# ScalarE's order of copies, exponentials and outputs in a decode attention kernel

## The chip, the cores and the metric

The kernel runs on one core of a Trainium2 chip. The metric is the time on the device in microseconds (us), the median of several runs. A core has engines that run side by side, each working through its own instructions in order: TensorE (PE in the profile), VectorE (DVE), ScalarE (ACT), GpSimd (POOL) and SyncE (SP), which here only issues transfers. They wait for each other through semaphores. Transfers between the chip's main memory and the core's own memory are made by 16 DMA engines.

## What is computed

One query for each of 16 heads attends to 8192 keys of width 256, all in bfloat16:

```python
B, H, Sq, Sk, D = 1, 16, 1, 8192, 256
scale = q.shape[-1] ** -0.5
scores = jnp.einsum("bhqd,bhkd->bhqk", q, k) * scale
p = _softmax(scores, axis=-1)
return jnp.einsum("bhqk,bhkd->bhqd", p, v)
```

K and V are 4 MiB a head each, 128 MiB (134.2 MB) together, and each is read once.

## The kernel before

A head's 8192 keys lie on 128 partitions, 64 keys to a partition, so K and V of a head are a tile of 128 x 64 columns of 256 numbers. There are two buffers for K and two for V, one for even and one for odd heads. SP issues the transfers in a fixed list (line 57): after the first heads always K of head h+2 and then V of head h. K of head h+2 waits until DVE and PE are through with K of head h (lines 132, 133); V of head h waits until the sum over V of head h-2 is done (line 135). V of heads 13 to 15 comes in pieces.

The scores of a head are split. DVE does 48 of the 64 columns, each a multiplication with q and a sum (line 189). PE and ACT do the other 16 in four groups of four columns: PE transposes a group (line 278), ACT copies it out of PE's memory (`evac`, line 367), PE multiplies it with q (line 292). `tp` and `KT` have two buffers each, so a group's transposes follow the scores of two groups before. ACT then copies the 16 columns of scores to the rest (`scopy`, line 371).

Around this stand, for each head: DVE's maximum over its columns (line 206), PE's transposition of it (226), DVE's maximum over the partitions (`xmax`, 173), PE's spreading of that over the partitions (`bcast`, 232), ACT's negation and exponential (`expo`, 375 and 379), which also makes the sum of each partition, PE's sum of these over the partitions (`total`, 242), DVE's reciprocal of it (`recips`, 178), PE's 64 multiplications of the weights with V (`pv`, 257), ACT's scaling of the result and the DMA issue of the output (`final`, 392 and 399). `q_copy` (362) lays the next head's q ready for DVE and PE; it waits until DVE is through with the head before, since there are two buffers.

All of it is written out by hand as loops over eight pairs of heads, one loop for each engine, and the order on an engine is the order of the text. PE's turn for the pair (even, odd) is: scores of the even head; pv of the previous even head, with the maximum, spreading and sum of the previous odd head at its columns 32, 48 and 64; scores of the odd head, with the maximum and spreading of the even head in between and its sum at the end; pv of the previous odd head. PE has a ninth turn for the last two pv. ACT's turn is, for the even and then the odd head: first copy, q copy, second copy, (odd head only: exponential of the even head), third and fourth copy, copy of the scores, (even head only: exponential of the previous odd head), and the output of the head two before. DVE's turn is the 48 columns of the even head, with `xmax` of the previous odd head at column 40, and the 48 of the odd head, with the reciprocal of the previous odd head at column 2, `xmax` of the even head at column 3, and the reciprocal of the even head at its end.

Semaphore values are counted from `AHEAD` (line 17), the number of steps that each is set to at the start; `of(1, 2)` is the head's number plus two. Both sums go to the same place (`qps`), and DVE reads it from there.

Of the kernel before, what the change touches and what calls it, by code (L numbers as in the profile page):

```python
# [13 lines left out]
K_FIRST = 16  # L14
V_HALVED = 13
V_LATE = {14: (0, 16, 32, 48), 15: (0, 16, 32, 44, 52, 58, 62)}
AHEAD = {"kd": 1, "sc": 1, "sp": 2, "ex": 2, "m": 1, "g": 1, "mT": 1, "l": 1, "bc": 1, "nb": 1, "rc": 2, "pv": 2, "fin": 4}
V_SEMS = (("va0", "v0b", "v0c", "v0d"), ("va1", "v1b", "v1c", "v1d", "v1e", "v1f", "v1g"))


# [20 lines left out]
def bass_standalone__mha_softmax__decode_kernel(nc: bass.Bass, q: bass.AP, k: bass.AP, v: bass.AP, out: bass.AP):  # L41
# [7 lines left out]
    NG = NPE // GRP  # L49
# [21 lines left out]
    with contextlib.ExitStack() as ctx:  # L71
# [9 lines left out]
        def sem(name):  # L81
            if name not in sems:
                sems[name] = ctx.enter_context(nc.semaphore(name))
            return sems[name]
# [39 lines left out]
        if True:  # L124
# [44 lines left out]
            @(lambda f: f(nc.vector))  # L169
            def _(dve):  # L170
                def xmax(h):
                    dve.wait_ge(sem("mT"), h.of(1, 2))
                    dve.tensor_reduce(g[0:1, h.par : h.par + 1], mx[0:1, 0:P], AX.X, ALU.max).then_inc(sem("g"), 1)  # L173

                def recips(h):
                    dve.wait_ge(sem("l"), h.of(1, 2))
                    dve.wait_ge(sem("fin"), h.of(1, 3))
                    dve.reciprocal(recip[0:1, h.par : h.par + 1], qps[0:1, 0:1]).then_inc(sem("rc"), 1)  # L178

                def head(h, at):  # L180
                    dve.wait_ge(sem("qb"), h.of(1, 1))
                    dve.wait_ge(sem("ex"), h.of(1, 1))
                    dve.wait_ge(sem(f"k{h.par}"), h.of(8, 16 - 8 * h.par))
                    buf = kbuf[h.par]
                    for j in range(JD):
                        if j == K_FIRST and h.par == 0:

                            dve.wait_ge(sem("k0b"), 16)
                        ins = dve.tensor_tensor_reduce(  # L189
                            out=buf[:, j * D : (j + 1) * D],  # L190
                            in0=buf[:, j * D : (j + 1) * D],
                            in1=q_now[h.par][:, 0:D],
                            scale=SCALE,
                            scalar=0.0,
                            op0=ALU.mult,
                            op1=ALU.add,
                            accum_out=S[h.par][:, j : j + 1],
                        )
                        if j in at:
                            at[j]()  # L200
                    ins.then_inc(sem("kd"), 1)
                    if JD in at:
                        at[JD]()
                    dve.wait_ge(sem("kd"), h.of(1, 2))
                    dve.wait_ge(sem("sc"), h.of(1, 2))
                    dve.tensor_reduce(m[:, h.par : h.par + 1], S[h.par][:, :], AX.X, ALU.max).then_inc(sem("m"), 1)  # L206

                with dve.Fori(0, H // 2) as i:
                    ev, od = _Step(0, i), _Step(1, i)
                    prev = od.back(2)  # L210

                    def later(f):
                        with dve.If(i > 0):
                            f(prev)

                    head(ev, {40: lambda: later(xmax)})
                    head(od, {2: lambda: later(recips), 3: lambda: xmax(ev), JD: lambda: recips(ev)})
                last = _Step(H - 1)
                xmax(last)
                recips(last)  # L220

            @(lambda f: f(nc.tensor))
            def _(pe):
# [16 lines left out]
                def total(h):  # L240
                    pe.wait_ge(sem("ex"), h.of(1, 3))
                    pe.matmul(  # L242
                        qps[0:1, 0:1],
                        lhsT=lsum[:, h.par : h.par + 1],
                        rhs=ones_col[:, 0:1],
                        start=True,
                        stop=True,
                    ).then_inc(sem("l"), 1)

                def pv(h, waits, at):  # L250

                    pe.wait_ge(sem("fin"), h.of(1, 3))
                    pe.wait_ge(sem(f"va{h.par}"), h.of(8, 32 - 8 * h.par))
                    for j in range(J):
                        for name, value in waits.get(j, ()):
                            pe.wait_ge(sem(name), value)
                        ins = pe.matmul(  # L257
                            acc[h.par][0:1, 0:D],
                            lhsT=E[h.par][:, j : j + 1],
                            rhs=vbuf[h.par][:, j * D : (j + 1) * D],  # L260
                            start=(j == 0),
                            stop=(j == J - 1),
                        )
                        if j == J - 1:
                            ins.then_inc(sem("pv"), 1)
                        if j + 1 in at:
                            at[j + 1]()
# [33 lines left out]
                def scores(t, before=None):  # L301
                    if before:
                        transpose_m(before)
                    for gi in range(NG):
                        ktrans(t, gi)
                        if gi >= 1:
                            kscore(t, gi - 1)
                        if gi == 1 and before:
                            bcast(before)
                    kscore(t, NG - 1)  # L310
                    if before:
                        total(before)

                pe.wait_ge(sem("ldq"), 16)
                pe.wait_ge(sem("cb"), 1)
# [23 lines left out]
                with pe.Fori(0, H // 2 + 1) as i:  # L339
                    ev, od = _Step(0, i), _Step(1, i)  # L340
                    fin_turn = pe.snap((i // 8) * 16 + 16)
                    half_turn = pe.snap(((i + 1) // 8) * 16 + 16)
                    old = od.back(2)
                    with pe.If(i < H // 2):
                        scores(ev)
                    with pe.If(i > 0):
                        pv(
                            ev.back(2),
                            {V_LATE[14][n]: [(V_SEMS[0][n], fin_turn)] for n in range(1, len(V_SEMS[0]))},
                            {32: lambda: transpose_m(old), 48: lambda: bcast(old), 64: lambda: total(old)},  # L350
                        )
                    with pe.If(i < H // 2):
                        scores(od, before=ev)
                    with pe.If(i > 0):
                        waits = {V_LATE[15][n]: [(V_SEMS[1][n], fin_turn)] for n in range(1, len(V_SEMS[1]))}
                        waits[HALF].append(("v1h", half_turn))
                        pv(old, waits, {})

            @(lambda f: f(nc.scalar))
            def _(act):  # L360
# [3 lines left out]
                def evac(h, gi):  # L364
                    act.wait_ge(sem("tp"), h.of(NG, gi + 1))
                    act.wait_ge(sem("sp"), h.of(NG, gi + 1))
                    act.activation(out=KT[gi % 2][:, :], in_=tp[gi % 2][:, :], func=ACT.Copy).then_inc(sem("kt"), 1)  # L367
# [54 lines left out]
                with act.Fori(0, H // 2) as i:  # L422
                    for c in (0, 1):
                        t = _Step(c, i)
                        evac(t, 0)
                        act.wait_ge(sem("kd"), t.of(1, 1))
                        act.wait_ge(sem("sp"), t.of(NG, 2))
                        q_copy(_Step(c + 1, i), q_all[:, bass.ds(i * (2 * QW) + (c + 1) * QW, QW)])
                        evac(t, 1)
                        if c:  # L430
                            expo(t.back(1))
                        evac(t, 2)
                        evac(t, 3)
                        scopy(t)
                        with act.If(i > 0):
                            if c == 0:
                                expo(t.back(1))
                            done = t.back(2)
                            at = nc.s_assert_within(
                                (i - 1) * (2 * D) + c * D,  # L440
                                0,
                                (H - 1) * D,
                                skip_runtime_bounds_check_because="the branch is taken from turn 1 on",
                            )
                            final(done, flat[:, bass.ds(at, D)])
                expo(_Step(H - 1))
                for h in (H - 2, H - 1):
                    final(_Step(h), out[0, h, 0:1, :])
# [31 lines left out]
```

## Time and profile before

| | |
|---|---|
| time, median of 3 runs | 321.04 us (320.5 to 322.54) |
| time of the profiled execution | 321.04 us |
| its span | 319.6 us |
| PE, DVE, ACT busy | 220.9, 274.9, 92.0 us (69%, 86%, 29%) |
| read from main memory | 134.23 MB, 420 GB/s over the span |
| granted TensorE clock, mean | 0.84 |

The profile is one execution. "Span" is the time from its first to its last instruction; the difference to the time lies around it. Busy time of an engine is an average over stages and does not say what sets the end; for that there are the chain of waits, which goes back from the last instruction to whatever released it each time, and the timeline, with the start and length of each instruction and the idle time before it. The granted clock is the share of TensorE's full clock that it was given. In rows of instructions, "L257" is line 257 of the kernel, "x64" the number of instructions merged into the row, and a pair of brackets the idle time before it and what ended it. SPq and ACTq are the queues that issue.

### The profile page before, as it was taken

Reading aid. Unit: us, or ns where it says so; the run is one execution under the profiler, and the core shown is the slowest. Engines: PE = TensorE matmul, PEld = TensorE weight load, DVE = VectorE, ACT = ScalarE, POOL = GpSimd, SP = SyncE. Lnnn points to the kernel's source line nnn. Section 1 sums busy time; section 2 is a strip of 40 time slices with the busy share of each in tenths; the row PEclk is TensorE's granted clock in tenths of the full one; section 3 lists DMA queues with packets and bytes.
Section 4 is the critical chain, followed back from the end, with each engine's and each line's share of the span. In section 5 each row is a group of like instructions: output and inputs, shape, how many; then the busy total and the mean of one; then the engine's idle time right before and its main releaser. Section 6 shows DMA issues by size and latency. Waiting matters only on the chain.

```text
span 319.6 us, 6845 instructions
## 1 busy us (share of the span) xinstructions
PE 220.9 (69%) x2162; PEld 156.3 (49%) x2162; DVE 274.9 (86%) x1584; ACT 92.0 (29%) x171; POOL 1.6 (0%) x11
## 2 busy tenths in 40 slices
PE   4427186797875947849297573966749477397997
PEld 1326154565554635626256352653626355265675
DVE  2799999999999998897979979889797997979910
ACT  5436050433224060510506123060231605116010
POOL 1000000000000000000000000000000000000000
PEclk9999999769598786969769598785969969587799
DMA  8999999999999999999999999999999999999994
GB/s 329 451 397 455 392 453 416 416 427 435 439 418 443 431 435 439 418 439 427 439 435 423 439 418 443 431 431 435 427 439 414 447 435 427 439 406 423 422 399 179
DMA packets 6549, 134.29 MB, mean 420 GB/s; under 512 B 752, under 2 KB 912, under 8 KB 1424
## 3 DMA queue, kind: packets, MB, share of 16 engines
q1 hardware_dynamic: 6480, 134.22, 98.3%
q8 instruction: 2, 0.03, 0.0%
q10 hardware_dynamic: 64, 0.02, 0.0%
q14 instruction: 3, 0.02, 0.0%
HBM read 134.23 MB, written 0.01 MB: 420 GB/s over the span
## 4 chain that ended last, share of the span: by engine, by line
DMA 49%; PE 24%; DVE 23%; issue 2%; ACT 1%; ACTq 0%; SPq 0%; DVEq 0%
DMA vbuf<-in_v_dram 45%; PE acc L257 23%; DVE kbuf L189 22%; DMA kbuf<-in_k_dram 4%; DVE S L189 1%; PE sm L232 1%; ACT KT L367 1%; PE mx L226 0%; ACT o_sb L392 0%; ACT q_now L362 0%; DVE g L173 0%; SPq L136 0%; PE spe L292 0%; ACTq L399 0%; DVE recip L178 0%
## 5 line engine op out<-in xcount | busy, mean ns | idle before, releaser
L189 DVE CUSTOM_DVE_ANT_0 kbuf<-kbuf,q_now 128x256 bf16<-128x256 bf16 x768 | 268.1, 413 | 22.2 <-DMA kbuf<-in_k_dram 21.2
L257 PE MATMUL acc<-vbuf,E 128*1 128x256 bf16 x1024 | 147.6, 315 | 36.3 <-DMA vbuf<-in_v_dram 36.3
L257 PEld LDWEIGHTS acc<-vbuf,E 128*1 128x1 bf16 x1024 | 96.7, 96 | 80.4 <-DMA vbuf<-in_v_dram 37.3
L367 ACT ACTIVATE KT<-tp 128x1024 bf16<-128x1024 bf16 x64 | 63.8, 1018 | 30.3 <-PE tp L278 30.1
L189 DVE DVE_READ_ACCUMULATOR2_ANT S<- 128x1 f32 x768 | 58.4, 76 | 0.0
L278 PE MATMUL tp<-identb,kbuf 128*128 128x128 bf16 x512 | 42.3, 239 | 13.9 <-DMA kbuf<-in_k_dram 13.8
L292 PE MATMUL spe<-q_now,KT 128*128 128x1 bf16 x512 | 23.1, 166 | 32.3 <-ACT KT L367 31.6
L278 PEld LDWEIGHTS tp<-identb,kbuf 128*128 128x128 bf16 x512 | 33.5, 107 | 18.3 <-DMA kbuf<-in_k_dram 12.4
L292 PEld LDWEIGHTS spe<-q_now,KT 128*128 128x128 bf16 x512 | 18.0, 100 | 42.0 <-ACT KT L367 32.0
L392 ACT ACTIVATE o_sb<-acc,recip 1x256 bf16<-1x256 f32 x16 | 7.4, 464 | 99.9 <-PE acc L257 98.6
L375 ACT ACTIVATE negb<-sm 128x1 f32<-128x1 f32 x16 | 2.8, 172 | 84.5 <-PE sm L232 84.5
L173 DVE TENSOR_REDUCE g<-mx 1x1 f32<-1x128 f32 x16 | 4.4, 276 | 9.8 <-PE mx L226 9.8
L226 PE MATMUL mx<-ident,m 128*1 128x128 f32 x32 | 6.3, 279 | 5.7 <-DVE m L206 5.7
L232 PE MATMUL sm<-g,ones_row 1*128 1x1 f32 x32 | 6.2, 262 | 4.1 <-DVE g L173 4.1
L232 PEld LDWEIGHTS sm<-g,ones_row 1*128 1x128 f32 x32 | 4.9, 190 | 6.2 <-DVE g L173 4.7
L362 ACT ACTIVATE q_now<-q_all 128x258 bf16 (+1 forms) x17 | 7.0, 412 | 0.3 <-DVE S L189 0.3
L178 DVE RECIPROCAL recip<-qps 1x1 f32<-1x1 f32 x16 | 2.4, 151 | 3.9 <-PE qps L242 3.9
L379 ACT ACTIVATE E<-S,negb 128x64 bf16<-128x64 f32 x16 | 5.6, 348 | 0.5
L226 PEld LDWEIGHTS mx<-ident,m 128*1 128x1 f32 x32 | 2.2, 83 | 6.3 <-DVE m L206 5.9
L329 PE MATMUL acc<-q_sb,identb 16*128 16x256 bf16 x16 | 4.4, 403 | 1.0 <-ACT q_all L412 1.0
L371 ACT ACTIVATE S<-spe 128x16 f32<-128x16 f32 x16 | 2.9, 183 | 7.3 <-PE spe L292 7.3
L412 ACT ACTIVATE q_all<-acc 128x512 bf16<-128x512 f32 x8 | 4.4, 593 | 0.9 <-PE acc L329 0.9
(20 smaller groups left out, 16.6 us busy)
## 6 DMA issues: line engine op xcount, KB each, us to landing
kbuf<-in_k_dram SPq DMA_DIRECT2D x15, 4096.0 KB, 20.5
vbuf<-in_v_dram SPq DMA_DIRECT2D x11, 4096.0 KB, 29.0
vbuf<-in_v_dram SPq DMA_DIRECT2D x6, 2048.0 KB, 24.4
vbuf<-in_v_dram SPq DMA_DIRECT2D x6, 1024.0 KB, 12.8
kbuf<-in_k_dram SPq DMA_DIRECT2D x1, 3072.0 KB, 11.7
kbuf<-in_k_dram SPq DMA_DIRECT2D x1, 1024.0 KB, 4.8
vbuf<-in_v_dram SPq DMA_DIRECT2D x1, 768.0 KB, 9.1
vbuf<-in_v_dram SPq DMA_DIRECT2D x1, 512.0 KB, 9.9
```

What stands on the lines that cost most here:

```text
L173: dve.tensor_reduce(g[0:1, h.par : h.par + 1], mx[0:1, 0:P], AX.X, ALU.max).then_inc(sem("g"), 1)
L189: ins = dve.tensor_tensor_reduce(out=buf[:, j * D : (j + 1) * D], in0=buf[:, j * D : (j + 1) * D], in1=q_now[h.par][:, 0:D], scale=SCALE, ...
L226: pe.matmul(mx[0:1, 0:P], lhsT=m[:, h.par : h.par + 1], rhs=ident[:, :], start=True, stop=True).then_inc(sem("mT"), 1)
L232: pe.matmul(sm[:, 0:1], lhsT=ones_row[0:1, 0:P], rhs=g[0:1, h.par : h.par + 1], start=True, stop=True,).then_inc(sem("bc"), 1)
L257: ins = pe.matmul(acc[h.par][0:1, 0:D], lhsT=E[h.par][:, j : j + 1], rhs=vbuf[h.par][:, j * D : (j + 1) * D], start=(j == 0), stop=(j == J ...
L278: ins = pe.transpose(tp[gi % 2][:, b * D + hf * P : b * D + (hf + 1) * P], buf[:, j * D + hf * P : j * D + (hf + 1) * P], identb[:, :],)
L292: ins = pe.matmul(spe[:, c : c + 1], lhsT=KT[gi % 2][:, b * D + hf * P : b * D + (hf + 1) * P], rhs=q_now[h.par][:, D + hf : D + hf + 1], ...
L329: ins = pe.matmul(acc[pair % 2][:, (h % 2) * D : (h % 2 + 1) * D], lhsT=identb[0:H, h : h + 1].to_broadcast([H, P]), rhs=q_sb[:, :], start ...
L362: act.activation(out=q_now[h.par][:, :], in_=src_q, func=ACT.Copy).then_inc(sem("qb"), 1)
L367: act.activation(out=KT[gi % 2][:, :], in_=tp[gi % 2][:, :], func=ACT.Copy).then_inc(sem("kt"), 1)
L379: act.activation(out=E[h.par][:, :], in_=S[h.par][:, :], func=ACT.Exp, bias=negb[:, h.par : h.par + 1], scale=1.0, accum_out=lsum[:, h.par ...
L392: act.activation(out=o_sb[h.par][0:1, :], in_=acc[h.par][0:1, 0:D], func=ACT.Copy, scale=recip[0:1, h.par : h.par + 1],).then_inc(sem("fin ...
```

## The change

On ACT, the four copies of a head come in one go; the exponential of the even head stands behind those of the odd head, the copy of the scores follows, and the q copy comes behind that. The output of the even head moves from the even head's place to the odd head's, so both outputs of the previous pair are issued at the end of the turn. On PE, the sum of the even head moves from the end of the odd head's scores to behind the pv of the previous odd head, in a branch of its own. On DVE, the reciprocal of the even head moves from the end of the odd head's columns to column 2 of the next even head, also in a branch, and after the loop for the last pair. The semaphore of the sums, `l`, is set one step further, so that its wait counts in the new order.

```diff
-AHEAD = {..., "l": 1, ...}
+AHEAD = {..., "l": 2, ...}
...
                 def recips(h):
-                    dve.wait_ge(sem("l"), h.of(1, 2))
+                    dve.wait_ge(sem("l"), h.of(1, 3))
...
-                    def later(f):
+                    def later(f, h):
                         with dve.If(i > 0):
-                            f(prev)
+                            f(h)
...
-                    head(ev, {40: lambda: later(xmax)})
-                    head(od, {2: lambda: later(recips), 3: lambda: xmax(ev), JD: lambda: recips(ev)})
+                    head(ev, {2: lambda: later(recips, ev.back(2)), 40: lambda: later(xmax, prev)})
+                    head(od, {2: lambda: later(recips, prev), 3: lambda: xmax(ev)})
                 last = _Step(H - 1)
+                recips(last.back(1))
                 xmax(last)
                 recips(last)
...
                     kscore(t, NG - 1)
-                    if before:
-                        total(before)
...
                         pv(old, waits, {})
+                    with pe.If(i < H // 2):
+                        total(ev)
...
                     for c in (0, 1):
                         t = _Step(c, i)
-                        evac(t, 0)
-                        act.wait_ge(sem("kd"), t.of(1, 1))
-                        act.wait_ge(sem("sp"), t.of(NG, 2))
-                        q_copy(_Step(c + 1, i), q_all[:, bass.ds(i * (2 * QW) + (c + 1) * QW, QW)])
-                        evac(t, 1)
+                        for gi in range(NG):
+                            evac(t, gi)
                         if c:
                             expo(t.back(1))
-                        evac(t, 2)
-                        evac(t, 3)
                         scopy(t)
+                        act.wait_ge(sem("kd"), t.of(1, 1))
+                        q_copy(_Step(c + 1, i), q_all[:, bass.ds(i * (2 * QW) + (c + 1) * QW, QW)])
                         with act.If(i > 0):
                             if c == 0:
                                 expo(t.back(1))
-                            done = t.back(2)
...
-                            final(done, flat[:, bass.ds(at, D)])
+                            else:
+                                for d in (0, 1):
...
+                                    final(t.back(3 - d), flat[:, bass.ds(at, D)])
```

More of the change, by code (lines that the diff above doesn't have):

```diff
@@ L16 @@
 V_LATE = {14: (0, 16, 32, 48), 15: (0, 16, 32, 44, 52, 58, 62)}
-AHEAD = {"kd": 1, "sc": 1, "sp": 2, "ex": 2, "m": 1, "g": 1, "mT": 1, "l": 1, "bc": 1, "nb": 1, "rc": 2, "pv": 2, "fin": 4}
+AHEAD = {"kd": 1, "sc": 1, "sp": 2, "ex": 2, "m": 1, "g": 1, "mT": 1, "l": 2, "bc": 1, "nb": 1, "rc": 2, "pv": 2, "fin": 4}
 V_SEMS = (("va0", "v0b", "v0c", "v0d"), ("va1", "v1b", "v1c", "v1d", "v1e", "v1f", "v1g"))
@@ L437, in _ @@
                                 expo(t.back(1))
-                            done = t.back(2)
[L439 to L444, printed above, removed]
-                            final(done, flat[:, bass.ds(at, D)])
+                            else:
+                                for d in (0, 1):
+                                    at = nc.s_assert_within(
+                                        (i - 1) * (2 * D) + d * D,
+                                        0,
+                                        (H - 1) * D,
+                                        skip_runtime_bounds_check_because="the branch is taken from turn 1 on",
+                                    )
+                                    final(t.back(3 - d), flat[:, bass.ds(at, D)])
                 expo(_Step(H - 1))
```

## The prediction

> **What bounds the kernel now.** I read the page first, then one window over nearly the whole run, then the DMA issues, and last the chain of waits from its end backwards.
>
> ```profile
> span 319.6 us, 6845 instructions
> ...
> q1 hardware_dynamic: 6480, 134.22, 98.3%
> ...
> DMA 49%; PE 24%; DVE 23%; issue 2%; ACT 1%; ACTq 0%; SPq 0%; DVEq 0%
> ...
> kbuf<-in_k_dram SPq DMA_DIRECT2D x15, 4096.0 KB, 20.5
> ...
> vbuf<-in_v_dram SPq DMA_DIRECT2D x1, 128.0 KB, 10.1
> ```
> ```profile
> 1.00:300.00 299.00, 203.00 (x2000) 142.84 (x2001) 270.43 (x1559) 90.03 (x165) 1.15 (x6) 0.83 1.00 429
> ```
>
> The last two columns of the window are the DMA share and GB/s: from 1 to 300 us the DMA engines are full at 429 GB/s. 134.22 MB at that rate are 312.9 us, so almost all of the 319.6 us is the stream of K and V. It is also well ahead of its need: a K of 4.19 MB takes 4.19/0.429 = 9.8 us, yet lands a median of 20.5 us after its issue, so about 10.7 us of other transfers stand in front of it. In the middle of the run a delay has to pass that cover before it costs anything. ACT is 1% of the chain, and a change in ACT's order can only count where the stream no longer sets the end. That place is found in the chain (start, length, what):
>
> ```profile
> 247.26 29.66 DMA vbuf<-in_v_dram
> ...
> 293.47 13.27 PE acc L257 x96
> ...
> 310.88 7.02 PE acc L257 x64
> 317.90 0.03 ACTq L391
> ...
> 317.98 0.47 ACT o_sb L392
> ```
>
> After the V of head 12 has landed at 276.9, no DMA stands in the chain. PE runs pv(12), the scores of head 15, and then 64+64+64 multiplications pv(13), pv(14), pv(15) without a gap, and the output follows. pv(15) takes 0.110 us a column (7.02/64), so it waits for none of its V pieces. What delays PE between 287 and 293.4 moves the end.
>
> **The change, part by part.** The scores of head 15 are that stretch, the ACT rows first and then PE's:
>
> ```profile
> 287.93 0.24 ACTq L399 DMA_DIRECT2D out_dram<-o_sb  x1
> 288.33 1.02 ACT L367 ACTIVATE KT<-tp 128x1024 bf16<-128x1024 bf16 x1 [0.58 <-PE tp L278]
> 289.25 0.41 ACT L362 ACTIVATE q_now<-q_all 128x258 bf16 x1
> 289.56 1.01 ACT L367 ACTIVATE KT<-tp 128x1024 bf16<-128x1024 bf16 x1
> 290.46 0.17 ACT L375 ACTIVATE negb<-sm 128x1 f32<-128x1 f32 x1
> ...
> 291.02 1.92 ACT L367 ACTIVATE KT<-tp 128x1024 bf16<-128x1024 bf16 x2
> ```
> ```profile
> 287.31 1.07 PE L278 MATMUL tp<-identb,kbuf 128*128 128x128 bf16 x16
> 289.41 0.35 PE L292 MATMUL spe<-q_now,KT 128*128 128x1 bf16 x8 [1.03 <-ACT KT L367]
> 289.69 0.38 PE L232 MATMUL sm<-g,ones_row 1*128 1x1 f32 x2
> 290.00 0.62 PE L278 MATMUL tp<-identb,kbuf 128*128 128x128 bf16 x8
> ...
> 290.84 0.61 PE L278 MATMUL tp<-identb,kbuf 128*128 128x128 bf16 x8
> ...
> 292.99 0.37 PE L292 MATMUL spe<-q_now,KT 128*128 128x1 bf16 x8 [0.54 <-ACT KT L367]
> 293.29 0.19 PE L242 MATMUL qps<-ones_col,lsum 128*1 128x1 f32 x2
> ```
>
> *The output of the even head leaves this place.* ACT issues the output DMA of head 12 until 288.17, and only then takes the first copy, at 288.33, although the first transposes began at 287.31. How early the copy could go is seen a turn before, where the output was done in time:
>
> ```profile
> 247.83 1.07 PE L278 MATMUL tp<-identb,kbuf 128*128 128x128 bf16 x16 [0.33 <-DMA kbuf<-in_k_dram]
> ```
> ```profile
> 248.49 1.02 ACT L367 ACTIVATE KT<-tp 128x1024 bf16<-128x1024 bf16 x1 [0.61 <-PE tp L278]
> ```
>
> That is 0.66 us behind the transposes, so 287.97 here: 0.36 us earlier. Both outputs, with their DMA issues, now come at the end of the odd head's turn; the even one is asked for by pv two heads later (line 252), a turn on, so nothing waits for it.
>
> *The q copy and the exponential leave the row of copies.* The q copy took 289.25 to 289.56, 0.31 us, and the exponential 290.46 to 291.02, 0.56 us. PE does not let all of that go, because a group's transposes follow the scores two groups before. I step it through from the first copy at 287.97. The scores of group 0 began 1.08 us behind it (289.41 less 288.33), so 289.05; the transposes of group 2 began 0.59 us behind those (290.00 less 289.41), so 289.64, and end 0.62 later at 290.26. With the 0.1 us that the first copy needed behind its eight transposes (0.66 less half of 1.07), copy 2 starts at 290.36, when copy 1 is long through. Copy 3 follows it 0.96 us on (half of the pair's 1.92; its transposes end 1.46 us behind those of group 2's start, 0.84+0.62, at 291.1), at 291.3. The old pair's second copy began at 291.98, and the last scores came 1.01 us behind that, at 292.99; so they now begin at 292.3. That is 0.67 us earlier in all. The bounds are 0.36 (only the output's delay goes) and 1.23 (0.36+0.31+0.56, if PE kept pace).
>
> *The sum of the even head moves behind pv(odd).* Line 242 takes 0.19 us, two instructions. At 293.29 it is largely hidden in the scores' end; now it stands between pv(13) and pv(14), with a branch of its own. No sum with a branch behind a pv shows alone; the nearest row is this one, so 0 to 0.19, and I take 0.1. Its wait is for the exponential of the even head, which ACT has done more than ten microseconds before, so PE does not stand.
>
> So PE's chain becomes 0.67-0.1 = 0.57 us shorter. Does the stream let that through?
>
> ```profile
> L136 SPq DMA_DIRECT2D vbuf<-in_v_dram x2: 450/450/451, 305.8 to 306.3; - x2
> ```
>
> The last piece of V, two columns, is issued at 306.3 and lands 10.1 us on, at 316.4; it is read by the last two multiplications, which begin at 317.9-2x0.11 = 317.7. PE may come 1.3 us earlier before it waits there. The first piece of this V is issued behind pv(13), which moves earlier too.
>
> *The middle and the start of the run.* The copies are faster there as well, but pv waits for V behind them, so I cost this at nothing; the cover is V's landing, and without it each pair would have the same half microsecond. The q copies come behind S's copy, some 4 us later than before; DVE wants them a head later. What is new is a wait on DVE: in the third column of every even head it takes the reciprocal of the even head before, and waits for the sum behind pv(odd). 45 more columns, and so the next K's issue, are queued behind it.
>
> ```profile
> 41.00 0.15 DVE L178 RECIPROCAL recip<-qps 1x1 f32<-1x1 f32 x1
> 41.11 0.22 DVE L206 TENSOR_REDUCE m<-S 128x1 f32<-128x64 f32 x1
> 41.83 0.43 DVE L189 CUSTOM_DVE_ANT_0 kbuf<-kbuf,q_now 128x256 bf16<-128x256 bf16 x1 [0.50 <-ACT q_now L362]
> ...
> 111.82 0.42 DVE L189 CUSTOM_DVE_ANT_0 kbuf<-kbuf,q_now 128x256 bf16<-128x256 bf16 x1 [0.68 <-DMA kbuf<-in_k_dram]
> ```
> ```profile
> 102.13 9.90 PE L257 MATMUL acc<-vbuf,E 128*1 128x256 bf16 x64 [1.96 <-DMA vbuf<-in_v_dram]
> ```
> ```profile
> 0.73 1.32 SPq L136 DMA_DIRECT2D kbuf<-in_k_dram  x3
> ...
> 58.73 0.33 SPq L136 DMA_DIRECT2D kbuf<-in_k_dram  x1
> ```
>
> Head 2 goes from 41.83 to the issue at 58.73, 16.9 us for 48 columns, 0.35 each. Head 6 starts at 111.82, so its third column is through near 112.9; pv(3) ends at 112.03 and the sum at 112.2. That is the pv of 9.9 us, a slow one, and it still leaves 0.7 us. The wait costs nothing, and the 10.7 us of cover stand behind it. The reciprocal itself moved the instruction after it by 0.11 us (41.00 to 41.11) and does so in either place. The added branch has no row of its own; the loop's edge, with its 0.50 us of idle time, is the widest step of DVE's program here, so 0 to 0.5 for each of eight even heads, hidden behind the wait for K that begins most heads. I take 0.
>
> The profiled execution's own time is 321.04 us, 1.44 more than its span, and equals the median of the three runs. 321.04-0.57 = 320.47.
>
> **The rivals.** *PE's clock returns sooner in pv(13).* The clock is the third column from the right:
>
> ```profile
> 292.00:293.00 1.00, 0.38 (x9) 0.31 (x10) 1.00 (x7) 0.93 (x2) 0.00 (x0) 0.56 1.08 459
> 293.00:298.00 5.00, 5.00 (x32) 3.09 (x33) 5.00 (x31) 0.18 (x1) 0.00 (x0) 0.50 0.98 413
> 298.00:299.00 1.00, 1.00 (x7) 0.57 (x5) 1.00 (x7) 0.00 (x0) 0.00 (x0) 0.53 1.00 418
> ```
> ```profile
> 238.00:241.00 3.00, 2.88 (x15) 1.75 (x16) 3.00 (x19) 0.00 (x0) 0.00 (x0) 0.51 1.01 437
> ```
> ```profile
> 238.12 5.00 PE L257 MATMUL acc<-vbuf,E 128*1 128x256 bf16 x32 [3.64 <-DMA vbuf<-in_v_dram]
> ```
>
> pv(13) runs at half clock from its start near 293.4 to 298.94 (0.53 is 94% of that microsecond at half), 5.5 us. The pv begun at 238.12 is back at full clock at 240.94, after 2.8 us. With 2.8 in place of 5.5, 2.7 us run at full speed, which is worth 1.35 us; with the 0.57 that would be 1.9, but the landing at 316.4 stops it at 1.3. The time would be 319.7. [...] If the clock came back at the same moment as now, the 0.57 us gained would be spent at half speed and be worth 0.28: 320.8, the forecast's upper end.
>
> [...]
>
> *The stream starves early (slower).* K of head 4 is issued at 58.73, when six whole heads of K or V, 25.2 MB, had been issued before it; at 429 GB/s from the first issue at 0.73 these end at 59.5. The cover there is under 1 us, not 10.7. Branches in heads 0 and 2 at 0.5 us each and the reciprocal at 0.15 would make DVE 1.15 us later; if the delay to a transfer's first bytes has already used the cover, the stream loses all of it: 320.47+1.15 = 321.6. It ends slower than before once more than 0.57 us goes this way. Against it: head 0's branch stands in its first 16 columns, behind which DVE waits for K anyway.
>
> *DVE's new wait bites.* Were pv(odd) all at half clock, 64x0.22 = 14.1 us in place of 9.9, DVE would stand 3.5 us in each even head; over the five later even heads 17.5 us, less the 10.7 of cover: about 6 us, 327. No pv in the trace is that slow.
>
> *Nothing comes through* because the end follows the stream after all: 321.0.
>
> **How the numbers follow.** The forecast has 0.62, with 319.9 (1.23 less 0.1) to 320.8 as its own range; the clock rival 0.14 (319.7), early starving 0.11 (321.6), nothing through 0.03, the wait on DVE 0.08, and 0.02 for a gain beyond what the landing allows. The last two are left out of the range, which spans the others and the scatter of 0.5 us that the runs show below their median: 319.2 to 322.0. Slower or faster by over 1% is about what a measurement can tell from no change, 3.2 us here; only the wait on DVE reaches it (0.08) and the unexplained gain (0.02), so 0.9 is within.
>
> **What would show it.** Right: in the scores of head 15 the first copy stands about 0.66 us behind the first transposes, the four copies stand together, PE's stretch from those transposes to the last scores is 5.0 us instead of 5.7, and GB/s from 1 to 300 us stays near 429. Wrong: idle time of DVE before line 178 put to PE's sum, a K issue with less than 10 us to its landing in the middle, a gap on PE between pv(13) and pv(14) over 0.2 us, or pv(15) waiting for V. A time under 319 or over 322 would mean that a term is missing.

## The result and the profile after

The changed kernel takes 320.22 us, the median of 18 runs (320.06 to 321.40). The kernel before took 321.03 us beside it, the median of 18 (320.44 to 322.54). The ratio is 0.9975, with a 95% interval from 0.9964 to 0.9986: a gain of 0.81 us, small but clear of the scatter. The forecast was 320.5 us.

The page of the changed kernel, its first line and its chain by engine, and below it the window from 1 to 300 us:

```profile
span 318.8 us, 6855 instructions
...
DMA 52%; DVE 23%; PE 22%; issue 1%; ACT 1%; SPq 0%; DVEq 0%; ACTq 0%
```
```profile
1.00:300.00 299.00, 199.50 (x2018) 142.72 (x2019) 270.58 (x1559) 90.50 (x165) 1.15 (x6) 0.84 1.00 429
```

The stream still runs at 429 GB/s with full DMA engines: the middle of the run is as it was, and 0.8 us of the span went at the end. DMA has risen from 49% to 52% of the chain and PE has fallen from 24% to 22%, which hints that the end has passed from PE to the stream. First the scores of head 15 on ACT, then PE from there on:

```profile
287.91 1.94 ACT L368 ACTIVATE KT<-tp 128x1024 bf16<-128x1024 bf16 x2 [2.01 <-PE tp L279]
290.24 1.94 ACT L368 ACTIVATE KT<-tp 128x1024 bf16<-128x1024 bf16 x2 [0.39 <-PE tp L279]
292.06 0.18 ACT L376 ACTIVATE negb<-sm 128x1 f32<-128x1 f32 x1
```
```profile
287.25 1.07 PE L279 MATMUL tp<-identb,kbuf 128*128 128x128 bf16 x16
...
292.23 0.37 PE L293 MATMUL spe<-q_now,KT 128*128 128x1 bf16 x8 [0.56 <-ACT KT L368]
292.56 8.52 PE L258 MATMUL acc<-vbuf,E 128*1 128x256 bf16 x64
300.92 0.19 PE L243 MATMUL qps<-ones_col,lsum 128*1 128x1 f32 x2
300.97 3.65 PE L258 MATMUL acc<-vbuf,E 128*1 128x256 bf16 x32
...
308.57 0.19 PE L243 MATMUL qps<-ones_col,lsum 128*1 128x1 f32 x2
308.92 1.91 PE L258 MATMUL acc<-vbuf,E 128*1 128x256 bf16 x16 [0.15 <-DMA vbuf<-in_v_dram]
311.41 5.68 PE L258 MATMUL acc<-vbuf,E 128*1 128x256 bf16 x48 [0.58 <-DMA vbuf<-in_v_dram]
```

The first copy stands 0.66 us behind the transposes, the four copies are together but for 0.39 us in which ACT waits for the third group's transposes, and the last scores begin 4.98 us behind the first transposes. In the profile before it was 5.68 us (292.99 less 287.31). pv(13) begins 5.31 us behind the transposes; it was 6.12.

What comes behind is new: pv(15) waits twice for V. The end of the chain says the same (start, length, what):

```profile
301.11 0.33 SPq L136
...
301.48 9.88 DMA vbuf<-in_v_dram
311.37 0.04 issue
311.41 1.91 PE acc L258 x16
313.32 0.12 issue
313.44 3.67 PE acc L258 x32
```

PE's rows at the same place in the kernel before:

```profile
310.69 0.19 PE L242 MATMUL qps<-ones_col,lsum 128*1 128x1 f32 x2
310.74 7.15 PE L257 MATMUL acc<-vbuf,E 128*1 128x256 bf16 x64
```

PE took the last head's sum, the step ahead of pv(15), at 308.57, where it had been at 310.69 before, so 2.1 us earlier; but the output starts at 317.18, where it had been at 317.98, only 0.8 us earlier. The rest went into waiting for V. Why PE was 2.1 us earlier and not 0.8 is in the clock, third column from the right:

```profile
292.00:293.00 1.00, 0.77 (x11) 0.56 (x12) 1.00 (x7) 0.97 (x6) 0.00 (x0) 0.50 1.12 475
293.00:298.00 5.00, 5.00 (x37) 3.42 (x36) 5.00 (x31) 0.52 (x2) 0.00 (x0) 0.76 0.97 408
```

0.76 over five microseconds is 2.4 us at half clock: the half clock lasts 3.4 us here, from 292.0 to 295.4, and lasted 6.8 us before, from 292.1 to 298.9. In this execution the clock came back after half that time, as the clock rival had it.

In these profiles the length goes with how soon pv(13) starts behind the clock's fall. In thirteen of the fourteen profiles of this study the clock falls in this stretch, between 290.9 and 293.2 us. Where pv(13) began at most 0.56 us behind the fall (here 0.56, in runs 6 and 8 below 0.09 and 0.04) the half clock lasted 3.4 us, and in the ten others, with 0.84 to 1.90 us, it lasted 6.8. pv(13) of run 6 and of the changed kernel's second profile, run 9, shows what that is worth on PE:

```profile
293.10 8.76 PE L258 MATMUL acc<-vbuf,E 128*1 128x256 bf16 x64
```
```profile
292.16 10.03 PE L258 MATMUL acc<-vbuf,E 128*1 128x256 bf16 x64
```

The three short ones all have the new order with the moved sum, which suggests that a shorter stretch can also bring the clock back 3.4 us sooner; but runs 1 and 9, with the same stretch, had the long one.

### The profile page after: what moved, and what is told of

Read it like the earlier page. It is cut to its first block, busy times and chain, and to the rows that moved or that the text cites. A ratio compares the mean times of both kernels' runs of the same rounds, so it can differ in the third digit from the quotient of the medians.

```text
span 318.8 us, 6855 instructions
## 1 busy us (share of the span) xinstructions
PE 215.7 (68%) x2162; PEld 154.4 (48%) x2162; DVE 275.1 (86%) x1584; ACT 92.5 (29%) x171; POOL 1.6 (0%) x11
## 4 chain that ended last, share of the span: by engine, by line
DMA 52%; DVE 23%; PE 22%; issue 1%; ACT 1%; SPq 0%; DVEq 0%; ACTq 0%
DMA vbuf<-in_v_dram 48%; DVE kbuf L189 22%; PE acc L258 20%; DMA kbuf<-in_k_dram 4%; DVE S L189 1%; PE sm L233 1%; ACT KT L368 1%; PE mx L227 0%; PE tp L279 0%; SPq L136 0%; PE spe L293 0%; DVE g L173 0%; ACT o_sb L393 0%; DVE recip L178 0%; DVEq L208 0%
## 5 line engine op out<-in xcount | busy, mean ns | idle before, releaser
L258 PE MATMUL acc<-vbuf,E 128*1 128x256 bf16 x1024 | 144.6, 310 | 45.2 <-DMA vbuf<-in_v_dram 45.1
L258 PEld LDWEIGHTS acc<-vbuf,E 128*1 128x1 bf16 x1024 | 94.8, 94 | 88.1 <-DMA vbuf<-in_v_dram 46.4
L368 ACT ACTIVATE KT<-tp 128x1024 bf16<-128x1024 bf16 x64 | 62.3, 1021 | 45.9 <-PE tp L279 45.4
L189 DVE DVE_READ_ACCUMULATOR2_ANT S<- 128x1 f32 x768 | 55.0, 72 | 0.0
L279 PE MATMUL tp<-identb,kbuf 128*128 128x128 bf16 x512 | 41.6, 236 | 13.6 <-DMA kbuf<-in_k_dram 13.4
```

The lines of the kernel that those rows point to most:

```text
L189: ins = dve.tensor_tensor_reduce(out=buf[:, j * D : (j + 1) * D], in0=buf[:, j * D : (j + 1) * D], in1=q_now[h.par][:, 0:D], scale=SCALE, ...
L258: ins = pe.matmul(acc[h.par][0:1, 0:D], lhsT=E[h.par][:, j : j + 1], rhs=vbuf[h.par][:, j * D : (j + 1) * D], start=(j == 0), stop=(j == J ...
L279: ins = pe.transpose(tp[gi % 2][:, b * D + hf * P : b * D + (hf + 1) * P], buf[:, j * D + hf * P : j * D + (hf + 1) * P], identb[:, :],)
```

## The experiments

Two questions were open. Where is the gain made: in the scores of head 15 alone, or a little in every pair? And what sets the end now: PE's chain, or the landing of the last V? Each kernel was run 8 to 12 times; "before" is the kernel before, run between them on the same chip. Its median there was 320.5 to 320.7 us, lower than the 321.03 of the first comparison, so ratios are to be compared rather than medians across groups. The ratios are not exactly those of the medians. The two columns in the middle are read from each kernel's own profile as above: from the first transposes of head 15 to the last scores, and to pv(13).

| kernel | to scores, us | to pv(13), us | median, us (range) | before, us | ratio (95% interval) |
|---|---|---|---|---|---|
| before | 5.68 | 6.12 | | | |
| changed | 4.98 | 5.31 | 320.22 (320.06-321.40) | 321.03 | 0.9975 (0.9964-0.9986) |
| changed, again | 4.98 | 5.31 | 320.40 (320.14-320.81) | 320.63 | 0.9989 (0.9977-1.0001) |
| 1 new order in the last turn only | 4.98 | 5.31 | 320.36 (320.16-320.68) | 320.70 | 0.9986 (0.9975-0.9997) |
| 2 new order in all turns but the last | 5.62 | 5.95 | 320.71 (320.19-321.60) | 320.70 | 0.9996 (0.9981-1.0012) |
| 3 changed, even output back | 5.34 | 5.67 | 320.62 (320.29-320.99) | 320.70 | 1.0000 (0.9989-1.0010) |
| 4 changed, sum and reciprocal back | 4.98 | 5.83 | 320.60 (320.18-321.26) | 320.70 | 0.9995 (0.9979-1.0010) |
| 5 before, even output moved | 5.31 | 5.80 | 320.47 (320.09-321.05) | 320.51 | 0.9993 (0.9979-1.0006) |

**1 and 2: the last turn alone, and all but the last.** Both keep the changed sums and reciprocals and hold the two orders of ScalarE side by side:

```diff
                 with act.Fori(0, H // 2) as i:
+                    with act.If(i < H // 2 - 1):
+                        ...
+                    with act.If(i > H // 2 - 2):
+                        ...
```

In the first the old order stands in the upper branch and the new one in the lower; in the second it is the other way round.

> ScalarE has the new order only in the last of its eight turns and the old one in the first seven; the sums and reciprocals stand as in the changed kernel. If the gain is made only where the scores of head 15 stand in PE's last chain, this gains all of it: 320.2 us, and the stretch from the transposes of head 15 to the start of pv(13) is 5.3 us as in the changed kernel (6.1 before). If each pair of heads gained a little, an eighth of it is left: 320.9 us.

> The complement: the new order on ScalarE in turns 0 to 6, the old one in the last turn, sums and reciprocals as in the changed kernel. Gain at the end only: nothing is left, 321.0 to 321.1 us, with the stretch at 6.0 us or more. Gain in each pair: seven eighths are left, 320.3 us.

The last turn alone gives 0.9986, as much as the changed kernel's 0.9989 beside the same kind of runs, and the same stretch of 5.31 us. The other seven turns give 0.9996, and their interval holds 1. The two intervals overlap, so it is the stretches that tell the two kernels apart, and the times agree with them. PE's rows of the second kernel at the end:

```profile
287.32 1.07 PE L279 MATMUL tp<-identb,kbuf 128*128 128x128 bf16 x16
...
292.94 0.37 PE L293 MATMUL spe<-q_now,KT 128*128 128x1 bf16 x8 [0.54 <-ACT KT L368]
293.27 9.53 PE L258 MATMUL acc<-vbuf,E 128*1 128x256 bf16 x64
302.64 0.19 PE L243 MATMUL qps<-ones_col,lsum 128*1 128x1 f32 x2
302.70 3.65 PE L258 MATMUL acc<-vbuf,E 128*1 128x256 bf16 x32
```

Since only the sum has moved at this place, the price of that move can be read here. From the last scores to pv(13) it is 0.33 us instead of 0.44, and between pv(13) and pv(14) the sum takes 0.06 us of PE's path. That is a gain of 0.05 us, where the prediction had put a loss of 0.1.

**3 and 5: the output's place, taken back and taken alone.** In the third kernel `final` of the even head stands again behind its own turn, in the fifth it is the only thing that is moved:

```diff
                             if c == 0:
                                 expo(t.back(1))
-                            else:
-                                for d in (0, 1):
-                                    ...
-                                    final(t.back(3 - d), flat[:, bass.ds(at, D)])
+                            done = t.back(2)
+                            ...
+                            final(done, flat[:, bass.ds(at, D)])
```

> The changed kernel with the even head's output back at the end of the even head's turn. By the step-through the first copy of head 15 comes 0.4 us later (0.66 to 1.0 us behind the transposes), and PE's stretch is 5.65 us. If the end is PE's, the time is 0.36 us more, 320.6; if the landing of the last V piece takes over, part of it is hidden, 320.3 to 320.5. If only the q copy and the exponential matter: 320.2 and no change of the stretch.

> The kernel before with nothing changed but the even head's output, moved to the odd head's end. The first copy of head 15 should come 0.36 us earlier and pv(13) with it: stretch 5.75 us, 320.7 us. If the output's place costs nothing: 321.0 us.

ACT's rows of the third kernel:

```profile
288.04 0.24 ACTq L400 DMA_DIRECT2D out_dram<-o_sb  x1
288.44 1.94 ACT L368 ACTIVATE KT<-tp 128x1024 bf16<-128x1024 bf16 x2 [0.58 <-PE tp L279]
```

The output's DMA issue stands ahead of the first copy again, and the copy is 1.01 us behind the transposes at 287.43. The output costs 0.36 us taken back (5.34 less 4.98) and saves 0.37 taken alone (5.68 less 5.31), both as the step-through had it. What is left, 0.33 or 0.34 us, belongs to the q copy and the exponential. The times are less sharp than the stretches: the third kernel is at 1.0000 and the fifth at 0.9993, and both intervals hold 1. The stretch is shown; what a part of it is worth in time these runs cannot separate.

**4: the sum in its old place.** The sums of `pe`, the reciprocals of `dve` and the count of `l` are as before, and ScalarE is as changed:

```diff
                     kscore(t, NG - 1)
+                    if before:
+                        total(before)
...
-                    with pe.If(i < H // 2):
-                        total(ev)
```

> The changed kernel with PE's sum of even heads and DVE's reciprocal of it back at their old places; the sum then waits on PE for the exponential behind the four copies, with pv(13) queued behind it. I expect pv(13) of the profile to start 0.4 us later behind the last scores (5.7 us of stretch), 320.3 to 320.6 us. If the sum's place is free of cost, 320.2 us and a stretch of 5.3 us.

```profile
293.03 0.19 PE L242 MATMUL qps<-ones_col,lsum 128*1 128x1 f32 x2 [0.16 <-ACT E L379]
293.34 13.53 PE L257 MATMUL acc<-vbuf,E 128*1 128x256 bf16 x96
```

The last scores begin at 292.49 as early behind the transposes as in the changed kernel, but then PE stands for the exponential, and pv(13) is queued behind it: 0.52 us of stretch are lost (5.83 less 5.31). So the sum's move is what lets the exponential go behind the copies; alone it is worth next to nothing.

**6 and 7: more work for PE ahead of pv(14).** Eight multiplications, added to the changed kernel and to the kernel before:

```diff
                     with pe.If(i < H // 2):
                         total(ev)
+                        for _ in range(8):
+                            pe.matmul(mx[0:1, 256 : 256 + D], lhsT=identb[0:H, 0:1], rhs=q_sb[:, :], ...)
```

> The changed kernel with eight more multiplications of 256 columns on PE at the end of each turn but the ninth, so also between pv(13) and pv(14); their result is not used. At full clock they take 8 x 0.11 = 0.88 us. If the end of the changed kernel is set by the landing of the last pieces of V, most of it is hidden: 320.2 to 320.6 us, and PE waits for V in pv(15) less or not at all. If the end is PE's own chain, 321.1 us.

> The same eight multiplications in the kernel before, whose end is PE's chain without a wait for V: the whole 0.88 us shows, 321.9 us. If the landing set its end too, 321.1 to 321.4 us.

The eight took 0.96 us on PE's path. The changed kernel with them is at 320.77 us (320.21 to 321.40), a ratio of 1.0006 (0.9995 to 1.0017), where the same kernel without had 0.9989 and, in the first comparison, 0.9975: 0.5 to 1.0 us more. In its profile pv(15) takes 7.15 us and does not wait for V. So the first expectation, nearly all hidden, did not come; whether a part is hidden these ratios do not tell. The kernel before with them is at 321.78 us (320.24 to 322.98), 1.27 above the 320.51 beside it and near its first expectation; but with runs spread over 2.7 us the ratio is 1.0023 (1.0001 to 1.0046), which leaves the size open. What the runs of the seventh add is their lower end. With almost a microsecond more for PE, its quickest run still takes 320.24 us. In all 130 runs of the kernel before in this study, 50 lie under 320.5 us and none under 320.0; of the 30 runs of the changed kernel, 23 lie under 320.5 us and none under 320.0. In these later groups the two kernels have the same floor: the change moves runs down to it, and does not lower it. The first comparison alone did not show this. There the quickest run of the kernel before took 320.44 us, that of the changed kernel 320.06, and under 320.5 us lay one of 18 against 15 of 18. Why the kernel before was slower in that group is not known.

**8: a longer last piece.** In the changed kernel, the last V in four pieces of 16 columns:

```diff
-V_LATE = {14: (0, 16, 32, 48), 15: (0, 16, 32, 44, 52, 58, 62)}
-V_SEMS = (("va0", "v0b", "v0c", "v0d"), ("va1", "v1b", "v1c", "v1d", "v1e", "v1f", "v1g"))
+V_LATE = {14: (0, 16, 32, 48), 15: (0, 16, 32, 48)}
+V_SEMS = (("va0", "v0b", "v0c", "v0d"), ("va1", "v1b", "v1c", "v1d"))
```

> The changed kernel with the last V in four pieces of 16 columns in place of seven pieces that end with 2. If the landing sets the end, 14 more columns stand behind the last landing: 14 x 0.11 = 1.5 us later at the same landing, less what PE waits now, 321.0 to 321.8 us, with PE waiting for V at column 48. If PE's chain sets the end: 320.2 us.

```profile
313.93 1.91 PE L258 MATMUL acc<-vbuf,E 128*1 128x256 bf16 x16 [0.72 <-DMA vbuf<-in_v_dram]
316.25 1.91 PE L258 MATMUL acc<-vbuf,E 128*1 128x256 bf16 x16 [0.41 <-DMA vbuf<-in_v_dram]
```

321.54 us (321.31 to 322.62), a ratio of 1.0036 (1.0021 to 1.0051). PE waits for the last 16 columns until 316.25 and has all of them still to do. The lowest run went up by 1.25 us, from 320.06 to 321.31: the floor is the landing of the last V and what PE has to do behind it. With the coarse pieces the last one set it. In the first profile of the changed kernel it was the second piece: it landed at 311.36 and 48 columns followed, while the last piece, 12.6 us behind its issue at 303.9, was there some 0.4 us before its two columns.

**9 to 12: is the spread the clock's?** The changed kernel again, and more multiplications on PE where it stands idle in the scores of odd heads, 5 ahead of the scores of group 0 and 4 ahead of groups 2 and 3:

```diff
                         ktrans(t, gi)
+                        if before and gi in (1, 3):
+                            warm(5 if gi == 1 else 4)
...
+                    if before:
+                        warm(4)
                     kscore(t, NG - 1)
```

In runs 10 and 11, `warm` multiplies 16 rows by one column (`q_sb` with a column of `identb`); in run 12 it uses the whole array (`q_all` with `identb`, 128 x 128).

> The changed kernel again, unaltered, beside the next two. If its runs end at a floor that the landing of the last V piece sets, the median is 320.2 and hardly a run is under 320.1; if PE's chain sets the end, its runs spread as those of the kernel before do, over some 2 us.

> The kernel before with 13 more multiplications of 256 columns in the idle places of PE in each odd head's scores (5 ahead of the scores of group 0, 4 ahead of groups 2 and 3), with results that nothing uses. If the clock's fall in pv(13) makes the spread of the kernel before and the landing is the floor under it, the clock stays at 1.00 in pv(13), pv(15) waits for V, and all runs are at 320.1 to 320.4 us without any change on ScalarE. If the clock falls nevertheless, or the spread has another cause, the median stays at 320.5 to 321.0 and the spread at 2 us.

> The same 13 multiplications in the changed kernel. With the landing as the floor there is nothing left to gain: 320.1 to 320.3 us, like the changed kernel, with the scattered runs over 320.4 gone. If PE's chain still set the end: 319.0 us or less.

> As the run before last but one (the kernel before with 13 more multiplications of 256 columns in the idle places of the odd heads' scores), with multiplications that use all 128 rows and columns of PE in place of 16 rows and one column; the result is not used. If the clock's fall ahead of pv(13) makes the spread of the kernel before, and if what the array does rather than PE's busy time decides the fall, the clock stays at 1.00 from 290 to 300, pv(13) takes 7.1 us, pv(15) waits for V, and the runs stand together at the landing's floor, 320.1 to 320.4 us, with nothing changed on ScalarE. If the clock falls as before: 320.6 to 321.0 us with a spread of 2 us.

The multiplications of the tenth and eleventh also lengthen the stretch to pv(13), to 6.37 us in the kernel before (6.12 without) and 5.60 in the changed one (5.31). The tenth did not do what it was for. Two of its windows:

```profile
290.00:292.00 2.00, 1.89 (x31) 1.26 (x30) 2.00 (x13) 1.97 (x6) 0.00 (x0) 0.97 0.98 418
...
293.00:298.00 5.00, 5.00 (x34) 3.00 (x33) 5.00 (x29) 0.18 (x1) 0.00 (x0) 0.50 0.97 406
```

PE was busy for 1.89 of the 2 us (the first number after the comma), and the clock fell all the same; 320.74 us (320.12 to 322.31), a ratio of 1.0006 (0.9989 to 1.0022), is the kernel before. In the eleventh the clock fell likewise, to 0.50 from 290.9 to 297.7 us. Its 320.49 us (320.02 to 321.01), a ratio of 0.9997 (0.9986 to 1.0007), shows only that no floor gives way; the runs over 320.4 us, which had been expected to go, are still there. In its profile the twelfth held the clock:

```profile
290.00:292.00 2.00, 1.80 (x33) 1.35 (x31) 2.00 (x12) 1.97 (x6) 0.00 (x0) 1.00 1.00 426
...
293.00:298.00 5.00, 4.69 (x42) 3.40 (x43) 5.00 (x31) 0.09 (x1) 0.00 (x0) 1.00 1.01 423
```
```profile
311.83 5.69 PE L257 MATMUL acc<-vbuf,E 128*1 128x256 bf16 x48 [0.57 <-DMA vbuf<-in_v_dram]
```

With ScalarE untouched, the order of the kernel before and a full clock bring PE to where it waits for V, at the same column as in the changed kernel. The median is 320.44 us (320.10 to 321.41) against 320.54, ratio 0.9990 (0.9975 to 1.0005). That is the changed kernel's 0.9989, but the interval holds 1, so what a full clock is worth in time is not shown. The profiled execution took 320.68 us with it, though pv(13), from its start to the next V's issue, takes 7.65 us (292.96 to 300.61) instead of 9.85 (293.43 to 303.28): the landing takes the rest. Its runs do not stand within 320.1 to 320.4, as I had expected; half are above. The landing is not at a fixed time either: in this profile the last piece of V lands 13.5 us behind its issue at 303.4, at 316.9, in the profile before at 316.4. What moves it was not tried.

So the question of the spread stays open in part. The profiles show one more source of it, ahead of everything that the change moves: PE does not reach head 15 at the same time. First the profile of run 11 (320.02 us), then that of run 7 (322.98 us):

```profile
286.61 1.07 PE L279 MATMUL tp<-identb,kbuf 128*128 128x128 bf16 x16
```
```profile
288.04 1.07 PE L278 MATMUL tp<-identb,kbuf 128*128 128x128 bf16 x16
```

Of the 1.43 us between them, 0.60 is the landing of the V of head 12 and 0.82 the first 32 columns of pv(12), which took 5.54 us in run 11 and 6.36 in run 7. The other twelve profiles lie between. In the profile of the kernel before and the first of the changed one these columns took 6.03 and 5.98 us, with a half clock that ended at 281.9 and 281.8.

The changed kernel's second profile is the counterpart to its first. Its clock was at 0.50 for the longer time, 6.8 us from 291.3 to 298.1, PE reached head 15 0.40 us earlier, and it still ended at the landing's edge:

```profile
293.00:298.00 5.00, 5.00 (x25) 2.99 (x24) 5.00 (x29) 0.12 (x1) 0.00 (x0) 0.50 0.97 408
```
```profile
309.74 7.25 PE L258 MATMUL acc<-vbuf,E 128*1 128x256 bf16 x64
```

pv(15) took 7.25 us instead of the 7.15 that the kernel before shows without a wait: PE and the landing arrive nearly together. With 3.4 or 6.8 us of half clock the changed kernel's two profiled executions took 320.24 and 320.14 us. In the profile of the kernel before PE never waits for V at the end, so there a longer half clock would add to the time; that is argued from the profile, not shown by a difference of times.

No kernel of these beats the changed one clearly.

## Why the prediction was right

*Where the gain is made.* The prediction put it into the scores of head 15, in PE's chain at the end, and nothing into the other seven pairs. The stretches of runs 1 and 2 show this, and their times agree: 0.9986 for the last turn alone, 0.9996, with an interval that holds 1, for the seven others.

*How large it is on PE.* 0.36 us for the output and 0.31 for the copies were stepped through, 0.67 together; the profiles show 0.36 to 0.37 and 0.33 to 0.34, 0.70 together. The bound of 1.23, all of what ACT no longer does there, was not reached for the reason given: ACT now waits 0.39 us for the third group's transposes, which follow the first group's scores.

*The sum's move* was mis-sized, by little: -0.1 us in the sum, +0.05 measured. The row that I took the price from holds two instructions that overlap with what follows; on PE's path the sum takes 0.06 us. And 0.11 us came back at its old place, which the prediction had called "largely hidden".

*PE's chain shorter by 0.57* thus became 0.75 us: 6.12 less 5.31 to pv(13), and 0.06 back for the sum behind it.

*Does the stream let it through?* Here the step was too generous. "PE may come 1.3 us earlier before it waits there" looked at the last piece alone; PE waited at the second piece, at column 16, because with the clock it was 2.1 us early. Of the prediction's own signs, those for right came (the first copy 0.66 us behind the transposes, a stretch of 5.0 us to the last scores, 429 GB/s), and so did one for wrong: pv(15) waiting for V. In that execution 0.8 us is what the landing left of 2.1, and not the sum of 0.57. More important, the prediction took the kernel before to be bound by PE at its end in every run. Fifty of 130 runs lay under 320.5 us, where the changed kernel's runs crowd, though only one of them in the first comparison. The gain is the mean of runs that had up to 2 us to lose and of runs that had none, and its agreement with a plain subtraction of 0.57 from the median is partly luck: in the first comparison it was 0.81 us, in the second 0.23.

*The rivals.* The clock's earlier return was seen in the first profile and not in the second (3.4 and 6.8 us of half clock), so it differs from run to run; that it would be stopped by the landing was right, but at 0.8 us and not at 1.3. Early starving did not come: K of head 4 was issued at 58.82 instead of 58.73. DVE's new wait did not bite; no idle time stands before its reciprocal in an even head.

## What to carry to other kernels

Where a stream sets the middle of a run, an order on a side engine counts in the last stage (here 0.9986 with it in the last turn alone, 0.9996 in the seven others), and that stage's own chain prices it well: two steps out of a row of copies were worth what the row let through, and not their own lengths. Before a gain at the end is counted, look for the next bound behind it, for each piece of the last transfer and not just the last; and look at the spread of the runs, since a common lower edge of two kernels points at a floor that no single profile shows. A step that is moved can need another one moved with it: the exponential behind the copies would have cost 0.5 us by the sum that waited for it.

## What was not expected of the hardware

When the added multiplications used 16 rows and one column, PE's clock fell to 0.50 although PE was busy: for 1.89 of the 2 us before in run 10, and for 2.96 of the 3 us before in run 11. It stayed at 1.00 in run 12, where as many multiplications used all rows and columns, with PE busy for 1.80 of 2 us. So in these runs PE's busy time, as the profile counts it, does not tell whether the clock falls. These are one execution of each, and the clock fell at another moment in runs 10 and 11 (291.9 and 290.9 us), so chance is not excluded.

The stream does not end sharply. In the changed kernel's profile the DMA engines are busy to 0.61, 0.42, 0.38 and 0.14 in the last four half microseconds from 314.0 to 316.0, with all pieces issued by 304.3. Why was not tried.
